# GpSimd's two-input elementwise work moved to VectorE, with new durations and priorities in the list scheduler

## The chip, the cores and the metric

The kernel runs on one core of a Trainium2 chip. A core has TensorE (matmuls, PE in the profile), VectorE (DVE), ScalarE (ACT), GpSimd (POOL) and SyncE (SP, which here issues every DMA). The metric is the time of one execution on the device in microseconds, as the median of several runs; lower is better.

## The reference

Three parts follow each other on 4 batches of 768 tokens with 8 heads of 48, which make a model width of 384. The first is an attention whose state decays by a complex number for each token and channel:

```python
mag = np.sqrt(a_re * a_re + a_im * a_im)
scale = np.minimum(mag, 0.999) / (mag + 1e-06)
for t in range(S):
    new_re = ar * S_re - ai * S_im
    new_im = ar * S_im + ai * S_re
    kv = np.einsum('bhd,bhe->bhde', k[:, :, t], v[:, :, t])
    S_re, S_im = (new_re + kv, new_im)
    y[:, :, t] = np.einsum('bhd,bhde->bhe', q[:, :, t], S_re)
```

The second mixes tokens by a product of rank 32 and applies a two-layer network of inner width 1536; the third gates by a causal convolution of 5 taps:

```python
h = xt @ U @ V
u = x + h.transpose(0, 2, 1)
x = u + np.maximum(u @ w_ch1, 0.0) @ w_ch2
gate = 1.0 / (1.0 + np.exp(-gate_pre))
out = gate * (x @ w_val) @ w_out
```

## The kernel before

**Recording and ordering.** `chunked_path` doesn't emit instructions as it is written. It records every instruction in a `Program` with its engine (V, G, A, P and S for VectorE, GpSimd, ScalarE, TensorE and SyncE), its inputs and outputs and an estimated duration. `order` then makes a list schedule: on the engine that is free first it takes the most urgent of what is ready. Urgency is the length of the remaining work, plus a number from the table `URGE` for the part of the program and the engine. `HOP` holds the estimated gaps between engines. The order of the planned starts becomes the program, and each engine runs its list strictly in that order. So the estimates cost no time themselves, but they decide who stands in front of whom. A two-input instruction `tt` of n elements a partition is planned at 142 + 2.1 n ns on GpSimd and 69 + n / 0.96 ns on VectorE.

**Attention.** A batch is taken in three units of 256 tokens (offsets 0, 256 and 512 in names such as `xa_1_256`). In each the decay is normalised (`xa`), prefix products are made by a row of `s` and `z` steps, and the two blocks of 8 tokens are then rotated: a product goes into `xc` (written `y2` in the code), two more into `z`, and a sum of both back into `z`. A later product of q and `z` goes into `xc` too (`qh`). Then come transposes (`pst`), scores (`pss`), masking (`mt`), state (`pkv`, `st`) and output (`py`).

**MoE.** Each batch has two halves of 384 tokens (names such as `xt_0_1` are batch and half). The matmuls run in a mode with truncated inputs, so every operand is split into a large and a small part by `pair`: ScalarE copies the large part, and a subtraction makes the small one. That happens to `m3u` (the input), `m3x` (the sum after the two layers), `m3g` (the gated value), three 128x384 tiles each, and to the 30 tiles of weights (`w`), after VectorE has made singles of doubles (`wt`). Between `px` (second layer) and `pv` (value product) lie VectorE's sum into `xt` and 12 steps `g` of the convolution. The `hp` tiles (hidden layer) are made by ScalarE and VectorE alone.

**Who does what.** Four constants choose an engine by batch: the rotation's product (`JE`) and the product with q (`QE`) go to GpSimd for batches 0 and 1; the subtraction of `pair` (`LE`) goes to GpSimd for batches 0 to 2; all of the weights' (`WE`) go to GpSimd. GpSimd else only writes constants at the start and one small memset a batch.

Of the kernel before, what the change touches and what calls it, by code (L numbers as in the profile page):

```python
# [100 lines left out]
class Program:  # L101
    """Records instructions, orders them for the in-order engines, then emits them."""

    # from the end of one instruction to the start of another that needs its result
# [8 lines left out]
    # what is added to the priority of the instructions of a part of the program on an engine  # L113
    URGE = {
        "a1A": 16000.0, "a1S": -10000.0, "a1V": -168000.0, "a3A": -8000.0, "a3V": -10000.0, "m0A": -2000.0,
        "m1A": -11000.0, "m1V": 283000.0, "m2A": -4000.0, "wA": -164000.0, "wG": -18000.0, "wS": -24000.0,
        "wV": -341000.0,
    }

    def hop(self, d, u):  # L120
        return self.HOP[d.eng + u.eng] if d.eng != u.eng or u.deps[d] else 0.0
# [61 lines left out]
    # TensorE runs at half of its clock after a tick in which too few columns left the array  # L183
# [14 lines left out]
    def lay(self, urgency, back=False):  # L198
        """List schedule (from the end if back): the most urgent of what is ready on the engine that is free first."""
# [6 lines left out]
        ready = [0.0] * len(ops)  # L206
# [53 lines left out]
# ---------------------------------------------------------------- the general path  # L260
def general_path(tc, q, k, v, a_re, a_im, moe_U, moe_V, w1, w2, w_val, conv_w, w_out, out):
    """Token by token, as the recurrence says; for decays and weights outside of what the chunked path may take."""
# [15 lines left out]
    with ExitStack() as ctx:  # L278
# [7 lines left out]
        with tc.tile_pool(name="ga", bufs=1) as ap, tc.tile_pool(name="gb", bufs=2) as bp:  # L286
# [10 lines left out]
            with tc.For_i(0, S, TB) as t0:  # L297
# [8 lines left out]
                # a min(|a|, .999) / (|a| + 1e-6); zero where |a|^2 overflows  # L306
# [44 lines left out]
        # weights: doubles to singles; beyond float32's range to zero and to infinity  # L351
# [121 lines left out]
# ---------------------------------------------------------------- the kernel  # L473
# [10 lines left out]
def chunked_path(ctx, tc, outer, q, k, v, a_re, a_im, moe_U, moe_V, w1, w2, w_val, conv_w, w_out, out):  # L484
    """Attention in chunks and the rest; returns 1 where the inputs allow it."""
# [36 lines left out]
    # instructions  # L522
# [56 lines left out]
    def matmul(o, lhsT, rhs, start=True, stop=True):  # L579
        n, m = rhs.free, lhsT.free  # L580
        passes = 1 if lhsT.probe.dtype == F32R else 4
        cost = 3 + (n / 2.4 if passes == 1 else max(n / 0.6, m / 0.6))
        op = g.add(
            "P", cost, lambda: nc.tensor.matmul(real(o), real(lhsT), real(rhs), start=start, stop=stop),  # L584
            views(lhsT, rhs), [o],
        )
        op.cols = passes * n * lhsT.shape[0] / 128
        return op

    def matmuls(o, parts, cost):  # L590
        """Products into disjoint columns of the array, side by side: (where in o, lhsT, rhs, start, stop)."""
# [17 lines left out]
    def dma(o, a, slow=1.0):  # L609
        """Slow: runs of less than 512 bytes."""  # L610
# [13 lines left out]
    JE, QE, LE, WE = ("GGVV", "GGVV", "GGGV", "G")  # L624
    # constants
# [28 lines left out]
    # weights  # L654
# [7 lines left out]
    def single(t, st):  # L662
        """t = float32 of the doubles in st (low word, high word), truncated to 24 bits."""
# [40 lines left out]
    def load_weights():  # L704
        """The doubles come to where their large and small parts will be."""
# [12 lines left out]
        for i, (to, key, *_) in enumerate(todo):  # L718
            x = T("p3", [128, PW], F32, "g", f"wt{i}")
            single(x, raw[i])  # L720
            to[key] = T("wts", [128, 2, PW], F32R, f"w{i}", f"w{i}")
            act(to[key][:, 0], x)
            sub(WE, to[key][:, 1], x, f32(to[key][:, 0]))

    xts, xus, yds, state, carry = {}, {}, {}, {}, {}
    # heads in pairs, each in 64 places: v, state and transposed output
# [9 lines left out]
    def attention(b, u0, R):  # L736
# [9 lines left out]
        # before the first MoE its places are free  # L746
# [4 lines left out]
        # normalisation of a  # L751
# [3 lines left out]
        for jb in range(NB):  # L755
# [4 lines left out]
            # a s, s = min(|a|, .999) / (|a| + 1e-6) = min(1, .999 r) (1 - 1e-6 r), r = 1 / |a|  # L760
# [18 lines left out]
        # prefix products inside the blocks of a row  # L779
# [12 lines left out]
        # products of rows as columns  # L792
# [14 lines left out]
        # (re, im) and (-im, re): what the parts of another factor are multiplied by  # L807
# [4 lines left out]
        # exclusive prefix over the rows; the unit starts from the phase of all before it  # L812
# [26 lines left out]
        # magnitude of the whole, and its phase as the next seed  # L839
# [30 lines left out]
        # P = prefix products; q P and -k / conj(P)  # L870
# [6 lines left out]
        for jb, (fj, fr, fi) in enumerate(fs_):  # L877
# [8 lines left out]
            mul(JE[b], y2, fj.unsqueeze(1).to_broadcast(ms), z[:, :, 1:2, :].to_broadcast(ms))  # L886
# [11 lines left out]
            mul(QE[b], qh, qk[:, 0].unsqueeze(2).to_broadcast(ms), z)  # L898
            mul("V", z, x0.unsqueeze(2).to_broadcast(ms), z)
            dma(kd[:, j0 * P2 : (j0 + RB) * P2], z.rearrange("p j c d -> p (j c d)"))  # L900
            # rows to columns
# [9 lines left out]
        # scores, state, output of each chunk  # L911
# [64 lines left out]
        # x^T U, a quarter of the columns in each group of lanes  # L976
# [19 lines left out]
    def pair(b, src, name, where=("p3", "m3")):  # L996
        t = T(where[0], [128, 2, TT], F32R, where[1], "m3" + name)
        act(t[:, 0], src)
        sub(LE[b], t[:, 1], src, f32(t[:, 0]))
        return t[:, 0], t[:, 1]  # L1000

    def moe(b):
# [106 lines left out]
    g.add("A", 1283.0, lambda: nc.scalar.preload_act_table_set(LN_EXP), [], [])  # L1109
    load_small()  # L1110
    def attend(b):
        g.kind = f"a{b}"
        t0 = 0
        for r in UNITS[b]:
# [11 lines left out]
    # the sum of all flags; anything but zero asks for the general path  # L1126
# [54 lines left out]
```

## Time and profile before

| | us |
|---|---|
| runs | 807.25, 811.2, 812.7; median 811.2 |
| span of the profiled execution | 805.2 |
| median of the runs less the span | 6.0 |
| VectorE busy | 652.5 |
| TensorE busy | 644.8 |
| ScalarE busy | 443.9 |
| GpSimd busy | 172.8 |

The time of the profiled execution itself is not listed beside the runs, so its span, with 6.0 us around it, stands for the median. An engine's busy time is the union of its instructions' spans; two instructions that follow each other on VectorE overlap by some tens of nanoseconds, so that durations add up to more than the busy time. TensorE's busy time includes stretches in which its clock was granted at less than full speed.

### The profile page before, as it was taken

Reading aid. Unit: us, or ns where it says so; the run is one execution under the profiler, and the core shown is the slowest. Engines: PE = TensorE matmul, PEld = TensorE weight load, DVE = VectorE, ACT = ScalarE, POOL = GpSimd, SP = SyncE. Lnnn points to the kernel's source line nnn. Section 1 sums busy time; section 2 is a strip of 40 time slices with the busy share of each in tenths; the row PEclk is TensorE's granted clock in tenths of the full one; section 3 lists DMA queues with packets and bytes.
Section 4 is the critical chain, followed back from the end, with each engine's and each line's share of the span. In section 5 each row is a group of like instructions: output and inputs, shape, how many; then the busy total and the mean of one; then the engine's idle time right before and its main releaser. Section 6 shows DMA issues by size and latency. Waiting matters only on the chain. (4 is left out here: it accounts for less than half of the span.)

```text
span 805.2 us, 12333 instructions
## 1 busy us (share of the span) xinstructions
PE 644.8 (80%) x4314; PEld 585.4 (73%) x4314; DVE 652.5 (81%) x1425; ACT 443.9 (55%) x1100; POOL 172.8 (21%) x139
## 2 busy tenths in 40 slices
PE   0001777858897699987998899889988999999985
PEld 0001666746787598885997799869977999799984
DVE  4989998999998988988989998999999837414361
ACT  6777875655365454575646654756466326413243
POOL 1363425225345412131003100220042003000000
PEclk9999755786999798998999999989999999999997
DMA  7687422530121324223212434131223330200000
GB/s 193 159 238 277 123 78 63 147 87 21 59 79 41 108 70 118 79 60 99 77 61 55 133 93 134 40 99 56 63 59 119 81 96 11 70 1 1 1 30 34
DMA packets 86885, 68.72 MB, mean 85 GB/s; under 512 B 52000, under 2 KB 79648, under 8 KB 86816
## 3 DMA queue, kind: packets, MB, share of 16 engines
q1 hardware_dynamic: 86816, 67.86, 29.2%
q8 instruction: 36, 0.59, 0.3%
q14 instruction: 33, 0.27, 0.1%
HBM read 48.97 MB, written 18.87 MB: 84 GB/s over the span
## 5 line engine op out<-in xcount | busy, mean ns | idle before, releaser
L584 PE MATMUL ph<-m3u,w 128*128 128x384 f32 x864 | 225.2, 363 | 14.4 <-DVE hp L551 5.2
L584 PE MATMUL px<-hp,w 128*128 128x384 f32 x864 | 201.3, 343 | 1.6 <-ACT hp L573 1.1
L584 PEld LDWEIGHTS ph<-m3u,w 128*128 128x128 f32 x864 | 160.8, 200 | 26.2 <-POOL m3u L535 8.9
L584 PEld LDWEIGHTS px<-hp,w 128*128 128x128 f32 x864 | 153.4, 189 | 3.8 <-ACT hp L573 2.0
L573 ACT ACTIVATE hp<-ph 128x384 fp32r<-128x384 f32 x96 | 46.6, 487 | 112.0 <-PE ph L584 111.6
L551 DVE SCALAR_TENSOR_TENSOR hp<-ph,hp 128x384 fp32r<-128x384 f32 x96 | 52.8, 551 | 59.6 <-ACT hp L573 59.3
L535 POOL TENSOR_TENSOR m3x<-xt,m3x 128x384 fp32r<-128x384 f32 x18 | 25.2, 1422 | 217.0 <-ACT m3x L573 211.4
L584 PE MATMUL pss<-qT,kT 96*128 96x128 f32 x384 | 61.3, 310 | 9.0 <-ACT qT L573 6.1
L535 DVE TENSOR_TENSOR s<-xa,z 128x192 f32<-128x192 f32 x168 | 63.9, 413 | 2.2 <-ACT z L573 1.4
L584 PEld LDWEIGHTS pss<-qT,kT 96*128 96x128 f32 x384 | 56.2, 219 | 12.4 <-ACT qT L573 7.3
L535 POOL TENSOR_TENSOR w<-wt,w 128x384 fp32r<-128x384 f32 x30 | 44.1, 1481 | 89.6 <-ACT w L573 89.6
L551 DVE SCALAR_TENSOR_TENSOR g<-xt,cw,g 128x384 f32<-128x384 f32 x96 | 62.2, 717 | 0.2 <-ACT g L573 0.2
L584 PE MATMUL pv<-m3x,w 128*128 128x384 f32 x216 | 50.4, 370 | 5.6 <-POOL m3x L535 3.3
L573 ACT ACTIVATE xa<-xa,cb 128x384 f32<-128x384 f32 x72 | 43.4, 610 | 15.9 <-DVE xa L551 10.3
L584 PE MATMUL po<-w,m3g 128*128 128x384 f32 x216 | 48.0, 354 | 3.7 <-POOL m3g L535 1.9
L605 PE MATMUL pst<-eye_r,xc 128*96 128x128 f32 x192 | 31.8, 298 | 19.9 <-POOL xc L535 19.2
L584 PEld LDWEIGHTS pv<-m3x,w 128*128 128x128 f32 x216 | 39.8, 204 | 8.7 <-POOL m3x L535 4.8
L605 PE MATMUL pst<-eye_r,z 128*96 128x128 f32 x192 | 31.0, 305 | 17.1 <-DVE z L535 11.9
L596 PE MATMUL py<-mt,vt 128*64 128x128 f32 x384 | 40.3, 302 | 4.1 <-DVE mt L535 3.7
L584 PEld LDWEIGHTS po<-w,m3g 128*128 128x128 f32 x216 | 37.0, 188 | 8.7 <-POOL m3g L535 3.5
L605 PEld LDWEIGHTS pst<-eye_r,xc 128*96 128x96 f32 x192 | 24.2, 138 | 23.5 <-POOL xc L535 19.3
L535 DVE TENSOR_TENSOR xa<-xa 128x384 f32<-128x384 f32 x48 | 28.4, 592 | 15.8 <-ACT xa L573 15.8
(157 smaller groups left out, 1282.3 us busy)
## 6 DMA issues: line engine op xcount, KB each, us to landing
raw<-in_moe_w_ch_dram SPq DMA_DIRECT2D x24, 384.0 KB
kd<-z SPq DMA_DIRECT2D x24, 384.0 KB
ks<-kd SPq DMA_DIRECT2D x20, 384.0 KB
ab<-in_a_re_dram SPq DMA_DIRECT2D x24, 192.0 KB
ab<-in_a_im_dram SPq DMA_DIRECT2D x24, 192.0 KB
qk<-in_k_dram SPq DMA_DIRECT2D x24, 192.0 KB
qk<-in_q_dram SPq DMA_DIRECT2D x24, 192.0 KB
vt<-in_v_dram SPq DMA_DIRECT2D x24, 192.0 KB
```

Of the source, the lines that this page charges most:

```text
L535: e, cost, lambda: engines[e].tensor_tensor(out=real(o), in0=real(a), in1=real(b), op=op), views(a, b), [o]
L551: lambda: nc.vector.scalar_tensor_tensor(out=real(o), in0=real(a), scalar=real(s), in1=real(b), op0=o0, op1=o1),
L573: return nc.scalar.activation(real(o), real(a), func, scale=real(scale), **kw)
L584: "P", cost, lambda: nc.tensor.matmul(real(o), real(lhsT), real(rhs), start=start, stop=stop),
L596: r = nc.tensor.matmul(ro[idx], real(lhsT), real(rhs), start=start, stop=stop)
L605: op = g.add("P", cost, lambda: nc.tensor.transpose(real(o), real(a), real(idn)), views(a, idn), [o])
```

## The change

The four constants are gone and `"V"` stands in the places where they chose: 108 two-input instructions (30 for `w`, 54 for `m3u`, `m3x` and `m3g` of batches 0 to 2, 24 for `xc` of batches 0 and 1) leave GpSimd's list for VectorE's. In the planner, a matmul of 384 columns is estimated at 174 ns where it was 163, the fp32 forms get 5 ns more, and a wait between two instructions of VectorE or of ScalarE that reuse a place counts 115 or 100 ns (`AGAIN`). The parts of the program are named more finely (a unit of attention, a half of the MoE, six weights), and `URGE` has 86 numbers for them where it had 13. Comments are gone. No instruction is added or removed, and no DMA.

```diff
+    AGAIN = {"V": 115.0, "A": 100.0}
     URGE = {
-        "a1A": 16000.0, "a1S": -10000.0, "a1V": -168000.0, "a3A": -8000.0, "a3V": -10000.0, "m0A": -2000.0,
...
+        "a00A": -3500.0, "a00P": 1500.0, "a00S": 6500.0, "a00V": 500.0, "a01A": -500.0, "a01P": -1000.0,
...
     def hop(self, d, u):
-        return self.HOP[d.eng + u.eng] if d.eng != u.eng or u.deps[d] else 0.0
+        return self.HOP[d.eng + u.eng] if d.eng != u.eng or u.deps[d] else self.AGAIN.get(d.eng, 0.0)
...
-        cost = 3 + (n / 2.4 if passes == 1 else max(n / 0.6, m / 0.6))
+        cost = 14 + n / 2.4 if passes == 1 else 8 + max(n / 0.6, m / 0.6)
...
-    JE, QE, LE, WE = ("GGVV", "GGVV", "GGGV", "G")
...
         for i, (to, key, *_) in enumerate(todo):
+            g.kind = f"w{i // 6}"
...
-            sub(WE, to[key][:, 1], x, f32(to[key][:, 0]))
+            sub("V", to[key][:, 1], x, f32(to[key][:, 0]))
...
-            mul(JE[b], y2, fj.unsqueeze(1).to_broadcast(ms), z[:, :, 1:2, :].to_broadcast(ms))
+            mul("V", y2, fj.unsqueeze(1).to_broadcast(ms), z[:, :, 1:2, :].to_broadcast(ms))
...
-            mul(QE[b], qh, qk[:, 0].unsqueeze(2).to_broadcast(ms), z)
+            mul("V", qh, qk[:, 0].unsqueeze(2).to_broadcast(ms), z)
...
-        sub(LE[b], t[:, 1], src, f32(t[:, 0]))
+        sub("V", t[:, 1], src, f32(t[:, 0]))
...
         for hf in range(NH):
             n = f"_{b}_{hf}"
+            g.kind = f"m{b}{hf}"
...
-        for r in UNITS[b]:
+        for i, r in enumerate(UNITS[b]):
+            g.kind = f"a{b}{i}"
```

The first place is the end of the second layer of MoE `_0_0` (batch 0, half 0). Before, GpSimd's list holds the small parts there, with a rotation's product of attention `_1_256` between them:

```order
L535 TENSOR_TENSOR m3x_0_0_2295<-xt_0_0_131,m3x_0_0_2295 128x384
L535 TENSOR_TENSOR m3x_0_0_2300<-xt_0_0_131,m3x_0_0_2300 128x384
L535 TENSOR_TENSOR m3x_0_0_2309<-xt_0_0_131,m3x_0_0_2309 128x384
L619 MEMSET xt_1_0_2351 128x3x4
L535 TENSOR_TENSOR xc_1_256_2406<-f3_1_256_2392,z_1_256_1833 128x8x96
L535 TENSOR_TENSOR m3g_0_0_2410<-g_0_0_2250,m3g_0_0_2410 128x384
L535 TENSOR_TENSOR m3g_0_0_2413<-g_0_0_2260,m3g_0_0_2413 128x384
L535 TENSOR_TENSOR m3g_0_0_2424<-g_0_0_2269,m3g_0_0_2424 128x384
```

and VectorE's list has the sum into `xt` and the convolution's steps, one behind the other:

```order
L535 TENSOR_TENSOR xt_0_0_131<-xt_0_0_131,px2_0_0_1738 128x384
L551 SCALAR_TENSOR_TENSOR g_0_0_2250<-xt_0_0_131,cw_308,g_0_0_2250 128x384
L551 SCALAR_TENSOR_TENSOR g_0_0_2260<-xt_0_0_131,cw_308,g_0_0_2260 128x384
L551 SCALAR_TENSOR_TENSOR g_0_0_2250<-xt_0_0_131,cw_308,g_0_0_2250 128x384
L551 SCALAR_TENSOR_TENSOR g_0_0_2269<-xt_0_0_131,cw_308,g_0_0_2269 128x384
L551 SCALAR_TENSOR_TENSOR g_0_0_2250<-xt_0_0_131,cw_308,g_0_0_2250 128x384
L551 SCALAR_TENSOR_TENSOR g_0_0_2260<-xt_0_0_131,cw_308,g_0_0_2260 128x384
L551 SCALAR_TENSOR_TENSOR g_0_0_2269<-xt_0_0_131,cw_308,g_0_0_2269 128x384
L551 SCALAR_TENSOR_TENSOR g_0_0_2260<-xt_0_0_131,cw_308,g_0_0_2260 128x384
L551 SCALAR_TENSOR_TENSOR g_0_0_2269<-xt_0_0_131,cw_308,g_0_0_2269 128x384
```

Now GpSimd's list holds only constants and memsets, and at the same place on VectorE the three subtractions stand among the convolution's steps:

```order
L551 TENSOR_TENSOR xt_0_0_92<-xt_0_0_92,px2_0_0_1751 128x384
L567 SCALAR_TENSOR_TENSOR g_0_0_2234<-xt_0_0_92,cw_336,g_0_0_2234 128x384
L567 SCALAR_TENSOR_TENSOR g_0_0_2238<-xt_0_0_92,cw_336,g_0_0_2238 128x384
L567 SCALAR_TENSOR_TENSOR g_0_0_2234<-xt_0_0_92,cw_336,g_0_0_2234 128x384
L567 SCALAR_TENSOR_TENSOR g_0_0_2238<-xt_0_0_92,cw_336,g_0_0_2238 128x384
L567 SCALAR_TENSOR_TENSOR g_0_0_2234<-xt_0_0_92,cw_336,g_0_0_2234 128x384
L567 SCALAR_TENSOR_TENSOR g_0_0_2238<-xt_0_0_92,cw_336,g_0_0_2238 128x384
L551 TENSOR_TENSOR m3x_0_0_2241<-xt_0_0_92,m3x_0_0_2241 128x384
L551 TENSOR_TENSOR m3x_0_0_2244<-xt_0_0_92,m3x_0_0_2244 128x384
L567 SCALAR_TENSOR_TENSOR g_0_0_2248<-xt_0_0_92,cw_336,g_0_0_2248 128x384
L567 SCALAR_TENSOR_TENSOR g_0_0_2234<-xt_0_0_92,cw_336,g_0_0_2234 128x384
L567 SCALAR_TENSOR_TENSOR g_0_0_2248<-xt_0_0_92,cw_336,g_0_0_2248 128x384
```

The first two `m3x` follow the sixth step of the convolution, the third follows the eleventh.

The second place is the rotation of attention `_1_256` on VectorE. Before, its product into `xc` was GpSimd's, and VectorE's list reads:

```order
L535 TENSOR_TENSOR t1_1_256_2426<-f3_1_256_2392,z_1_256_1833 128x192
L535 TENSOR_TENSOR xa_1_512_2046<-ab_1_512_2196,xa_1_512_2046 128x8x96
L535 TENSOR_TENSOR z_1_256_1833<-f3_1_256_2392,z_1_256_1833 128x8x48 x2
L535 TENSOR_TENSOR fb_1_256_2454<-t1_1_256_2426 128x96
L535 TENSOR_TENSOR z_1_256_1833<-z_1_256_1833,xc_1_256_2406 128x768
```

Now the products into `xc` of both blocks stand among the others:

```order
L551 TENSOR_TENSOR xc_1_256_2413<-f3_1_256_2386,z_1_256_1771 128x8x96
L551 TENSOR_TENSOR st0_132<-pkv_1_0_1_2400,st1_128 96x8x48
L551 TENSOR_TENSOR t1_1_256_2426<-f3_1_256_2386,z_1_256_1771 128x192
L567 SCALAR_TENSOR_TENSOR xa_1_512_2048<-xa_1_512_2048 128x8x48
L551 TENSOR_TENSOR z_1_256_1771<-f3_1_256_2386,z_1_256_1771 128x8x48
L551 TENSOR_TENSOR fb_1_256_2438<-t1_1_256_2426 128x96
L551 TENSOR_TENSOR z_1_256_1771<-f3_1_256_2386,z_1_256_1771 128x8x48
L551 TENSOR_TENSOR xa_1_512_2048<-ab_1_512_2227,xa_1_512_2048 128x8x96
L551 TENSOR_TENSOR xc_1_256_2459<-fb_1_256_2438,z_1_256_1771 128x8x96
L551 TENSOR_TENSOR xt_0_1_1656<-xt_0_1_1656,pu_0_1_2472 128x384
L551 TENSOR_TENSOR z_1_256_1771<-z_1_256_1771,xc_1_256_2413 128x768
```

Two products of 128x768 have moved in between (`xc` from `f3` and from `fb`), ahead of the sum that reads the first of them.

On TensorE's list the order of the stages stays: the first matmul of MoE `_0_0` stands 50.2 us of matmul work from the list's start in both kernels and the first of MoE `_3_0` 484.8 us, where work is counted as each matmul by the shortest duration of its form in the trace.

## Rows read from the trace of the kernel before

**Rows 1.** The page: busy time, share of the span and instructions of each engine.

```profile
PE 644.8 (80%) x4314; PEld 585.4 (73%) x4314; DVE 652.5 (81%) x1425; ACT 443.9 (55%) x1100; POOL 172.8 (21%) x139
```

**Rows 2.** Windows: length, then PE, PEld, DVE, ACT, POOL busy, clock, DMA share, GB/s.

```profile
0.00:190.00 190.00, 86.12 (x555) 71.23 (x555) 169.73 (x393) 128.51 (x367) 70.95 (x66) 0.81 0.51 147
190.00:690.00 500.00, 456.67 (x3187) 415.67 (x3186) 436.58 (x939) 274.42 (x643) 101.84 (x74) 0.96 0.27 77
690.00:806.00 116.00, 102.03 (x574) 98.48 (x573) 46.16 (x95) 40.98 (x92) 0.00 (x0) 0.96 0.07 22
620.00:690.00 70.00, 69.10 (x544) 64.43 (x542) 40.64 (x79) 28.08 (x57) 6.64 (x6) 1.00 0.23 64
```

**Rows 3.** GpSimd's groups by form: count, busy us, mean ns, idle before, releasers.

```profile
L535 POOL TENSOR_TENSOR m3x<-xt,m3x 128x384 fp32r<-128x384 f32 x18 | 25.2, 1422 | 217.0 <-ACT m3x L573 211.4 <-DVE g L551 5.6
```

**Rows 4.** Timeline at 274 us: start, duration, engine, instruction.

```profile
274.43 1.82 POOL L535 TENSOR_TENSOR xc<-qk,z 128x768 f32<-128x768 f32 x1 [1.24 <-DVE xc L551]
...
274.74 1.73 DVE L535 TENSOR_TENSOR z<-s,s 128x192 f32<-128x192 f32 x1
```

**Rows 5.** VectorE's groups by form, whole run.

```profile
L535 DVE TENSOR_TENSOR s<-xa,z 128x192 f32<-128x192 f32 x168 | 63.9, 413 | 2.2 <-ACT z L573 1.4
...
L551 DVE SCALAR_TENSOR_TENSOR g<-xt,cw,g 128x384 f32<-128x384 f32 x96 | 62.2, 717 | 0.2 <-ACT g L573 0.2
...
L551 DVE SCALAR_TENSOR_TENSOR hp<-ph,hp 128x384 fp32r<-128x384 f32 x96 | 52.8, 551 | 59.6 <-ACT hp L573 59.3
...
L535 DVE TENSOR_TENSOR z<-s,s 128x192 f32<-128x192 f32 x84 | 35.7, 425 | 0.6
...
L535 DVE TENSOR_TENSOR z<-xc,z 128x768 f32<-128x768 f32 x24 | 23.6, 984 | 3.6 <-POOL xc L535 3.4
...
L535 DVE TENSOR_TENSOR z<-f,z 128x384 f32<-128x384 f32 x24 | 20.3, 844 | 3.7 <-POOL xc L535 3.4
...
L535 DVE TENSOR_TENSOR m3u<-xt,m3u 128x384 fp32r<-128x384 f32 x6 | 3.3, 554 | 1.6 <-ACT m3u L573 1.6
...
L563 DVE TENSOR_SCALAR fine<-f 1x1 int32<-1x1 f32 x1 | 0.1, 142 | 7.1 <-ACT f L573 7.1
```

**Rows 6.** VectorE's groups by form, 380 to 420 us, where GpSimd is idle.

```profile
L551 DVE SCALAR_TENSOR_TENSOR hp<-ph,hp 128x384 fp32r<-128x384 f32 x12 | 6.6, 548 | 0.2 <-ACT hp L573 0.2
...
L535 DVE TENSOR_TENSOR s<-xa,z 128x192 f32<-128x192 f32 x14 | 4.5, 352 | 0.8 <-ACT z L573 0.6
...
L535 DVE TENSOR_TENSOR z<-s,s 128x192 f32<-128x192 f32 x7 | 2.5, 353 | 0.2
...
L535 DVE TENSOR_TENSOR xc<-qk,z 128x768 f32<-128x768 f32 x2 | 1.9, 958 | 0.1
...
L535 DVE TENSOR_TENSOR z<-f,z 128x384 f32<-128x384 f32 x1 | 0.5, 546 | 0.0
```

**Rows 7.** VectorE's groups by form, 740 to 790 us, after GpSimd's last instruction.

```profile
L551 DVE SCALAR_TENSOR_TENSOR g<-xt,cw,g 128x384 f32<-128x384 f32 x23 | 12.5, 612 | 0.0
```

**Rows 8.** TensorE's groups by form, whole run.

```profile
L584 PE MATMUL ph<-m3u,w 128*128 128x384 f32 x864 | 225.2, 363 | 14.4 <-DVE hp L551 5.2 <-POOL m3u L535 4.7 <-ACT m3u L573 4.0
...
L584 PE MATMUL pv<-m3x,w 128*128 128x384 f32 x216 | 50.4, 370 | 5.6 <-POOL m3x L535 3.3 <-DVE m3x L535 1.3 <-ACT ob L573 0.8
...
L584 PE MATMUL po<-w,m3g 128*128 128x384 f32 x216 | 48.0, 354 | 3.7 <-POOL m3g L535 1.9 <-ACT m3g L573 1.7
```

**Rows 9.** Timeline around the end of `px` of MoE `_0_0`.

```profile
242.25 6.43 DVE L551 SCALAR_TENSOR_TENSOR g<-xt,cw,g 128x384 f32<-128x384 f32 x12
...
245.43 6.61 POOL L535 TENSOR_TENSOR m3x<-xt,m3x 128x384 fp32r<-128x384 f32 x3 [6.30 <-ACT m3x L573]
...
249.59 2.29 PE L584 MATMUL pv<-m3x,w 128*128 128x384 f32 x6 [3.31 <-POOL m3x L535]
```

**Rows 10.** The chain that ended last, near 715 us: start, us, what.

```profile
713.50 0.52 PE px L584 x3
```

**Rows 11.** Timeline at 185 us: the first layer of MoE `_0_0` begins.

```profile
185.68 4.53 PE L584 MATMUL ph<-m3u,w 128*128 128x384 f32 x13 [1.24 <-POOL m3u L535]
```

More of the change, by code (lines that the diff above doesn't have):

```diff
@@ L111 @@
     }
+    AGAIN = {"V": 115.0, "A": 100.0}
     URGE = {
-        "a1A": 16000.0, "a1S": -10000.0, "a1V": -168000.0, "a3A": -8000.0, "a3V": -10000.0, "m0A": -2000.0,
-        "m1A": -11000.0, "m1V": 283000.0, "m2A": -4000.0, "wA": -164000.0, "wG": -18000.0, "wS": -24000.0,
-        "wV": -341000.0,
[16 rows of a table added]
     }
     def hop(self, d, u):
-        return self.HOP[d.eng + u.eng] if d.eng != u.eng or u.deps[d] else 0.0
+        return self.HOP[d.eng + u.eng] if d.eng != u.eng or u.deps[d] else self.AGAIN.get(d.eng, 0.0)
     def __init__(self, nc):
@@ L1109, in chunked_path @@
     g.add("A", 1283.0, lambda: nc.scalar.preload_act_table_set(LN_EXP), [], [])
+    g.kind = "s"
     load_small()
     def attend(b):
-        g.kind = f"a{b}"
         t0 = 0
-        for r in UNITS[b]:
+        for i, r in enumerate(UNITS[b]):
+            g.kind = f"a{b}{i}"
             attention(b, t0, r)
```

15 rows, old and new, of the table URGE are left out of this document.

## The prediction

> **What bounds the kernel now.** I read the page's shares first, then windows by stage, then the groups of GpSimd and VectorE, then the timeline where both work. By the page no engine is full: VectorE 81%, TensorE 80%, GpSimd 21% [rows 1]. By stages it looks different [rows 2]. Up to 190 us (weights and the first attention) VectorE is busy for 169.7 of 190 us and TensorE for 86.1: VectorE sets the end of this stage. From 690 us (the MoE of batch 3) TensorE is busy for 102.0 of 116 us, and VectorE for 46.2: TensorE sets it. In the middle, 500 us long, TensorE has 456.7 and VectorE 436.6; there they take turns, and only its last 70 us are plainly TensorE's (69.1 of 70). The middle is where an idle TensorE can be won back: it has 43.3 us without a matmul, and a granted clock of 0.96.
>
> The second thing to see is that VectorE's own durations are not constant. At 274.43 us GpSimd begins a product of 1.82 us; a VectorE sum `z<-s,s` that begins 0.3 us later lasts 1.73 us and ends with it, within a quarter of a microsecond [rows 4]. In a stretch without work on GpSimd that same form takes 353 ns [rows 6]. Over the whole run forms with two SBUF inputs are longer than in quiet stretches: `s` 413 against 352 ns, `z<-s,s` 425 against 353, `z<-f,z` 844 against 546 [rows 5, 6], `g` 717 against 612 [rows 5, 7]. `hp`, which reads one input from PSUM, keeps its 551 against 548 [rows 5, 6]. So a GpSimd instruction often holds up one VectorE instruction until it ends, where both read two tensors in SBUF.
>
> The Trainium skill says the same of the cause (SBUF — State Buffer, Who interferes with whom): a VectorE instruction with two SBUF inputs and a GpSimd instruction that reads SBUF contend for one shared port, and whichever comes second is blocked wholly. By that rule, the trace agrees, 1.73 us for the blocked sum.
>
> **The change, part by part.**
>
> *What VectorE gains back.* Four forms alone: `s` 168 x (413 - 352) = 10.2 us, `g` 96 x (717 - 612) = 10.1, `z<-s,s` 84 x (425 - 353) = 6.0, `z<-f,z` 24 x (844 - 546) = 7.2, in sum 33.6 [rows 5 to 7]. The same subtraction over all 57 forms (1425 instructions, from `s` to `fine` [rows 5]), each against the median of its instructions that no GpSimd arithmetic overlaps, gives 79 us: 27 in instructions that start before 190 us, 53 in the middle, nothing after. That is 0.73 us for each of GpSimd's 108 two-input instructions.
>
> *What VectorE gets.* 84 subtractions of 128x384 at 554 ns (the six that VectorE did already [rows 5]) are 46.5 us; 24 products of 128x768 at 958 ns [rows 6] are 23.0. Neighbours overlap: all durations add up to 739 us where VectorE was busy for 652.5 [rows 1], which is 0.06 us for each of 1425. So 69.5 - 108 x 0.06 = 63.0 us of new busy time. Net: 63 - 79 = -16 us; VectorE's work becomes smaller though it takes over GpSimd's.
>
> *First stage.* Ahead of the first `xt` sum of MoE `_0_0`, VectorE's new list holds 46 more instructions, 29.0 us by their durations, 26 after overlap; 27 come back. Its waits for GpSimd's products ahead of `z`, 3.4 and 3.4 us [rows 5], vanish as waits, since the products are its own now. The weight loads are issued in another order and the V tables first; VectorE has other work meanwhile, and I cost that at nothing (without this cover it is the few DMA issues that move ahead, some 2 us). In sum -6 or so; I take -5.
>
> *Middle.* 63 - 26 = 37 us come, 53 go: -16 on VectorE in 500 us. It shows only where VectorE is the later one; the bounds are 0 and all 16. TensorE has 43.3 us without a matmul and is otherwise busy, so I take two thirds, -11.
>
> *Boundaries of the MoE.* 18 groups of three subtractions (`m3u`, `m3x`, `m3g`, two halves, three batches) stand between ScalarE's large part and TensorE. In MoE `_0_0` the three took GpSimd 6.61 us beside the twelve `g`, and TensorE waited 3.31 us for the second of them [rows 9]. In the new order two stand behind the sixth `g` and one behind the eleventh: 13 instructions of some 0.53 us (6.43 us for twelve [rows 9]) and the third is done 7 us after the first `g` begins, where it was 9.8 (245.43 + 6.61 - 242.25). By the means [rows 3, 5] a group lasts 3 x 0.55 = 1.7 us in place of 3 x 1.42 = 4.3 (`m3x`'s mean). Fully exposed that were 18 x 2.6 = 47 us; TensorE's waits that name GpSimd come to 4.7 + 3.3 + 1.9 = 9.9 us [rows 8], the other bound is 0, where each subtraction waits behind VectorE's instruction in progress as long as it gains. I take -7, near the waits.
>
> *Planner.* The old table planned a matmul of 384 columns at 163 ns; the chain shows three in 0.52 us, 173 each [rows 10], the new estimate. VectorE's plan held no blocking at all, so 79 us of its time fell outside the plan, and what stood next in its list need not have been what TensorE missed most. What a plan that fits better is worth the profile of before doesn't show; bounds are +15 (an order fitted to the plan and not to the chip) and -15 (about a third of the 43.3 us [rows 2]). I take -3.
>
> *Last stage.* Batch 3's subtractions were VectorE's already and TensorE sets the pace: 0. The lists of TensorE differ there only in how `pv` and `po` of one half stand among the other's matmuls.
>
> Sum: -5 - 11 - 7 - 3 = -26 us. The span of 805.2 stands for the median of 811.2, with 6.0 around it; so **785 us**.
>
> **The rivals.**
>
> *More: the idle time in the middle is halved* (chance 0.18). If all of VectorE's 16 us show, the waits of 9.9 us go, the first stage gives 6 and the plan and the clock (0.96 over 500 us [rows 2]) another 14, that is -46: 765. For it: where TensorE idles in the middle, VectorE is mostly busy. Against: both were near full, and only one order can suit both.
>
> *Hidden* (0.12). TensorE holds the middle and VectorE's relief turns into idle time. For it: the last 70 us of the middle [rows 2]. Against: 43.3 us without a matmul. Between -10 and 0: 801 to 811, about 808.
>
> *Slower, by the queue on VectorE* (0.05). GpSimd could start a subtraction as soon as ScalarE's part was there; on VectorE it stands at a planned place behind the convolution or a unit of attention. Place: the same 18 groups. Price: if each comes as much as 2.8 us later (five `g` of 0.54 us in front, as before the third `m3x`), 18 x 2.8 = 50 us, 811 - 26 + 50 = 835. It decides from 26 / 18 = 1.4 us a group. Against: in the place that I followed the third came earlier.
>
> *Slower, because VectorE is full* (0.05). If its long instructions had another cause than GpSimd, nothing comes back and 63 us come on top. VectorE is idle for 20 us in the first stage and 63 in the middle [rows 2], of which 29 lie in the last 70 us; with some 28 of the 63 us taken up there, 35 remain: 846. It decides where less than about half of the 79 us comes back. Against: `hp` does not lengthen.
>
> The Trainium skill has a rule that leans this way (Perfetto Trace Analysis, Optimizing Scalar/DVE Operations): where VectorE is saturated, moving work to other engines, even to GpSimd, may make sense; it adds that between these two it might not help, because of the port. Taken alone, the first half speaks for the old split.
>
> That the change does not do what it says is excluded: the new list has the 108 on VectorE and only memsets and constants on GpSimd.
>
> **How the numbers follow.** Forecast 785 (0.60, by itself 773 to 797), more 765 (0.18), hidden 808 (0.12), the two slower ones 0.05 each. A change of 1% (8 us) is about what a measurement of this kernel can tell. Faster by over 1%: 0.60 + 0.18 + a third of the hidden case, 0.82. Within 1%: the rest of it and the edge of the slower ones, 0.09. Slower: 0.09. The range leaves out about 0.07 below, and above it the slower cases and a little of the hidden one: 765 to 806.
>
> **What would show it.** VectorE's busy time falls to some 636 us with 108 more instructions; `s`, `g` and `z` come to 352, 612 and 350 to 546 ns everywhere. The first layer of MoE `_0_0` begins at about 181 us, where it was 185.7 [rows 11]. TensorE's idle time in the middle falls below 30 us, and the stage from 190 to 690 us shrinks to about 480. The last stage stays at 116. I am wrong if VectorE's durations stay long without GpSimd, if new waits of TensorE for `m3u`, `m3x` or `m3g` on VectorE pass 25 us, or if the middle keeps its length with VectorE idler.

## The result and the profile after

The changed kernel takes 775.11 us (median of 4 runs, 772.76 to 778.13) where the kernel before took 809.23 beside it (4 runs): ratio 0.9572, 95% interval 0.9533 to 0.9611. Its profiled execution took 775.49 us with a span of 773.7, so that 1.8 us lie around the span.

Page of after, first part, for [rows 1]:

```profile
PE 627.6 (81%) x4314; PEld 578.4 (75%) x4314; DVE 626.0 (81%) x1533; ACT 442.7 (57%) x1100; POOL 2.7 (0%) x31
```

VectorE executes 108 more instructions and is busy for 26.5 us less; GpSimd falls from 172.8 to 2.7 us. TensorE is busy for 17.2 us less with the same 4314 matmuls.

Windows of after, for [rows 2], same columns:

```profile
0.00:190.00 190.00, 82.92 (x556) 69.89 (x557) 166.73 (x442) 131.93 (x374) 2.33 (x28) 0.82 0.51 147
190.00:690.00 500.00, 473.07 (x3364) 438.20 (x3363) 425.42 (x1027) 280.45 (x662) 0.32 (x3) 0.98 0.28 79
```

Between 190 and 690 us TensorE has 26.9 us without a matmul, where it had 43.3, and fits 177 matmuls more into the same 500 us.

VectorE's groups of after by form, whole run, for [rows 5]:

```profile
L551 DVE TENSOR_TENSOR s<-xa,z 128x192 f32<-128x192 f32 x168 | 54.8, 355 | 4.3 <-ACT z L589 3.9
L567 DVE SCALAR_TENSOR_TENSOR g<-xt,cw,g 128x384 f32<-128x384 f32 x96 | 53.1, 617 | 0.2 <-ACT g L589 0.2
L567 DVE SCALAR_TENSOR_TENSOR hp<-ph,hp 128x384 fp32r<-128x384 f32 x96 | 53.0, 554 | 59.1 <-ACT hp L589 58.5
...
L551 DVE TENSOR_TENSOR z<-s,s 128x192 f32<-128x192 f32 x84 | 29.9, 355 | 0.3
...
L551 DVE TENSOR_TENSOR z<-f,z 128x384 f32<-128x384 f32 x24 | 13.3, 553 | 0.0
```

Every form has in the whole run, to about 1%, the duration that it had before in stretches without GpSimd [rows 6, 7]; `hp` stays where it was.

TensorE's groups of after by form, for [rows 8]:

```profile
L600 PE MATMUL ph<-m3u,w 128*128 128x384 f32 x864 | 215.0, 355 | 8.5 <-ACT m3u L589 3.9 <-DVE hp L567 3.0 <-DVE m3u L551 1.3
...
L600 PE MATMUL pv<-m3x,w 128*128 128x384 f32 x216 | 53.0, 372 | 6.4 <-DVE m3x L551 3.6 <-ACT m3x L589 2.0 <-ACT ob L589 0.8
L600 PE MATMUL po<-w,m3g 128*128 128x384 f32 x216 | 51.1, 355 | 0.0
```

The waits for a small part came to 9.9 us on GpSimd; on VectorE they are 1.3 + 3.6 + 0. Of the 3.6 us, 1.4 belong to batch 3, whose small parts were VectorE's already and cost 1.3 us then [rows 8]; for batches 0 to 2 it is 9.9 us before and 3.5 after.

**Where the time went.** I cut the spans where TensorE has done the same work in both kernels, to a few matmuls, and to whole microseconds: up to the first layer of MoE `_0_0`; from there to that of `_1_0`; to that of `_3_0`; to the end. Windows of before:

```profile
0.00:181.00 181.00, 79.47 (x537) 65.89 (x537) 160.76 (x377) 125.22 (x358) 63.90 (x61) 0.82 0.53 152
181.00:374.00 193.00, 166.46 (x1080) 148.80 (x1080) 177.20 (x381) 104.64 (x255) 63.47 (x41) 0.90 0.26 74
374.00:695.00 321.00, 300.61 (x2153) 274.71 (x2153) 271.33 (x586) 176.78 (x409) 45.42 (x38) 0.98 0.27 78
695.00:805.00 110.00, 98.29 (x545) 95.98 (x545) 43.17 (x84) 37.27 (x81) 0.00 (x0) 0.96 0.05 18
```

and of after:

```profile
0.00:185.00 185.00, 77.92 (x538) 65.04 (x539) 161.73 (x427) 128.63 (x367) 2.33 (x28) 0.83 0.53 151
185.00:350.00 165.00, 152.10 (x1081) 139.41 (x1082) 157.48 (x396) 102.60 (x248) 0.11 (x1) 0.98 0.30 85
350.00:664.00 314.00, 299.97 (x2155) 278.23 (x2155) 264.11 (x630) 174.92 (x408) 0.22 (x2) 0.97 0.29 81
664.00:774.00 110.00, 97.58 (x544) 95.71 (x542) 42.63 (x83) 36.56 (x80) 0.00 (x0) 0.95 0.04 14
```

The first stretch became 4 us longer, the second 28 shorter, the third 7 shorter; the last kept its length. The 28 have two halves: TensorE is idle for 12.9 us instead of 26.5, and busy for 152.1 instead of 166.5 with the same matmuls, at a granted clock of 0.98 instead of 0.90.

### The profile page after: what moved, and what is told of

Its sections match the earlier page's. It is cut to its first block, busy times and chain, and to the rows that moved or that the text cites. A ratio compares the mean times of both kernels' runs of the same rounds, so it can differ in the third digit from the quotient of the medians.

```text
span 773.7 us, 12227 instructions
## 1 busy us (share of the span) xinstructions
PE 627.6 (81%) x4314; PEld 578.4 (75%) x4314; DVE 626.0 (81%) x1533; ACT 442.7 (57%) x1100; POOL 2.7 (0%) x31
## 4 chain that ended last, share of the span: by engine, by line
PE 48%; DVE 25%; DMA 13%; ACT 7%; issue 3%; SPq 2%; ACTq 0%; DVEq 0%
PE ph L600 14%; PE px L600 12%; DMA ab<-in_a_im_dram 5%; PE pv L600 5%; DVE xc L551 4%; PE py L612 4%; DVE z L551 4%; PE pss L600 3%; PE po L600 3%; PE pkv L612 3%; DVE g L567 3%; DVE s L551 3%; DVE xa L551 2%; DMA raw<-in_moe_w_ch_dram 2%; SPq L631 2%
## 5 line engine op out<-in xcount | busy, mean ns | idle before, releaser
L600 PE MATMUL ph<-m3u,w 128*128 128x384 f32 x864 | 215.0, 355 | 8.5 <-ACT m3u L589 3.9
L600 PE MATMUL px<-hp,w 128*128 128x384 f32 x864 | 206.2, 344 | 0.2 <-ACT hp L589 0.2
L600 PE MATMUL pss<-qT,kT 96*128 96x128 f32 x384 | 59.0, 301 | 5.2 <-ACT qT L589 5.2
L551 DVE TENSOR_TENSOR s<-xa,z 128x192 f32<-128x192 f32 x168 | 54.8, 355 | 4.3 <-ACT z L589 3.9
L600 PE MATMUL pv<-m3x,w 128*128 128x384 f32 x216 | 53.0, 372 | 6.4 <-DVE m3x L551 3.6
L567 DVE SCALAR_TENSOR_TENSOR g<-xt,cw,g 128x384 f32<-128x384 f32 x96 | 53.1, 617 | 0.2 <-ACT g L589 0.2
L600 PE MATMUL po<-w,m3g 128*128 128x384 f32 x216 | 51.1, 355 | 0.0
L621 PE MATMUL pst<-eye_r,xc 128*96 128x128 f32 x192 | 31.8, 293 | 19.9 <-DVE xc L551 17.2
L621 PE MATMUL psT<-eye_r,qd 128*96 128x128 f32 x24 | 5.3, 305 | 45.8 <-ACT qd L589 43.0
L612 PEld LDWEIGHTS pkv<-vt,ks 128*96 128x96 f32 x320 | 34.5, 188 | 5.4 <-issue 3.8
L589 ACT ACTIVATE xa<-ab 128x768 f32<-128x768 f32 x24 | 20.2, 842 | 31.3 <-DMA ab<-in_a_im_dram 21.9
```

Of the source, the lines that this page charges most:

```text
L551: e, cost, lambda: engines[e].tensor_tensor(out=real(o), in0=real(a), in1=real(b), op=op), views(a, b), [o]
L567: lambda: nc.vector.scalar_tensor_tensor(out=real(o), in0=real(a), scalar=real(s), in1=real(b), op0=o0, op1=o1),
L589: return nc.scalar.activation(real(o), real(a), func, scale=real(scale), **kw)
L612: r = nc.tensor.matmul(ro[idx], real(lhsT), real(rhs), start=start, stop=stop)
L621: op = g.add("P", cost, lambda: nc.tensor.transpose(real(o), real(a), real(idn)), views(a, idn), [o])
```

## The experiments

Theory A (the prediction's): GpSimd's two-input instructions held up VectorE's, and without them VectorE's time comes back, whatever the plan. B: the new plan makes the gain. C: the small parts come later because of VectorE's queue, and something else makes up for it. D: the small parts reach TensorE sooner because VectorE needs 0.55 us for one. Ratios are to the kernel before, run beside each on the same chip; "lengthening" is the sum over VectorE's instructions of their duration less the median of those of the same form that no GpSimd arithmetic overlaps, 79 us before and 0 after.

**e1_old_order_on_dve.** The kernel before with its own plan; only the engine that executes the 108 is another, each at the place where its planned start put it.

```diff
-            e, cost, lambda: engines[e].tensor_tensor(out=real(o), in0=real(a), in1=real(b), op=op), views(a, b), [o]
+            e, cost, lambda: nc.vector.tensor_tensor(out=real(o), in0=real(a), in1=real(b), op=op), views(a, b), [o]
```

> The kernel before with its plan and the lists of TensorE, ScalarE and SyncE untouched; the 108 two-input instructions that were GpSimd's stand at the same places of the program but are VectorE's. If the blocking by GpSimd is what was lost (theory A), VectorE's forms come to their quiet durations (s 352, g 612 ns), its busy time falls by 10 to 25 us, and the time comes to 785 to 797 although nothing was planned for it. If the new plan is what gained (rival B), the time stays at 805 to 815. If VectorE's queue is a loss that the plan has to hide (rival C), it is above 820.

Measured: 776.91 us, ratio 0.9598 [0.9542, 0.9655], lengthening 0, VectorE busy for 630.9 us. Windows, cut as above:

```profile
0.00:172.00 172.00, 75.87 (x537) 63.22 (x537) 155.35 (x408) 125.01 (x358) 2.34 (x28) 0.92 0.56 160
172.00:354.00 182.00, 164.06 (x1080) 148.50 (x1080) 166.27 (x423) 105.61 (x256) 0.11 (x1) 0.90 0.27 78
354.00:670.00 316.00, 299.88 (x2154) 275.28 (x2155) 266.47 (x623) 177.12 (x410) 0.22 (x2) 0.98 0.28 80
```

The move alone gives the whole gain within the intervals, and 8 us more than A expected at best; B falls as its cause. The way there is another: the first stretch gets 9 us shorter and not 4 longer, the second 11 and not 28, and the clock of the second stays at 0.90.

**e2_new_order_on_gpsimd.** The changed kernel's plan, with the 108 executed by GpSimd at the places that the plan gave them on VectorE.

```diff
-        cost = 142 + 2.1 * n if e == "G" else 69 + n / 0.96
+        cost = 69 + n / 0.96
-            e, cost, lambda: engines[e].tensor_tensor(out=real(o), in0=real(a), in1=real(b), op=op), views(a, b), [o]
+            "V", cost, lambda: engines[e].tensor_tensor(out=real(o), in0=real(a), in1=real(b), op=op), views(a, b), [o]
...
-            sub("V", to[key][:, 1], x, f32(to[key][:, 0]))
+            sub("G", to[key][:, 1], x, f32(to[key][:, 0]))
...
-        sub("V", t[:, 1], src, f32(t[:, 0]))
+        sub("GGGV"[b], t[:, 1], src, f32(t[:, 0]))
```

> The changed kernel with its plan and the lists of TensorE, ScalarE and SyncE untouched; the same 108 instructions go back to GpSimd at their places. Theory A: VectorE's two-input forms lengthen by some 60 to 80 us in all, TensorE waits for m3u, m3x and m3g on GpSimd, and the time comes to 800 to 825. Rival B: it stays at 773 to 785, since the order is the new one. Rival C: it is at or under 775, since VectorE has 63 us less to do.

Measured: 810.43 us, ratio 1.0023 [0.9986, 1.006], lengthening 71 us. The new order without the move is worth nothing; the move on it is worth 1.0023 - 0.9572 = 0.045, on the old order 0.040.

**e3_move_replanned.** The kernel before with `"V"` in the four constants, planned anew with the old durations and priorities.

```diff
-    JE, QE, LE, WE = ("GGVV", "GGVV", "GGGV", "G")
+    JE, QE, LE, WE = ("VVVV", "VVVV", "VVVV", "V")
```

> The kernel before with its four constants set to VectorE, planned again with the old durations and old priorities. Theory A: 780 to 797, most of the gain. Rival B: 803 to 815.

Measured: 836.90 us, ratio 1.0336 [1.0298, 1.0374], with lengthening 0; neither A nor B had expected a loss of this size. It shows most in the stretch from MoE `_0_0` to `_0_1`:

```profile
175.00:303.00 128.00, 106.96 (x617) 96.50 (x617) 121.86 (x315) 72.49 (x176) 0.11 (x1) 0.76 0.25 74
```

It was 90 us long before and 73 after. VectorE, busy for 121.9 of the 128 us, is given work of attention in front of MoE `_0_1`: 318.8 us of its durations start ahead of that first layer, in the changed kernel 281.6. TensorE has work of other parts in the stretch too, 617 matmuls where before has 447, so that not all of its length is lost. Over equal work the loss is spread: from `_0_0` to `_1_0` it takes 216 us (193 before, 182 in e1), from there to `_3_0` 334 us (321 and 316). The same move that gains 4% on the old order loses 3% when the planner may react to it with this table.

**e4_plan_only.** The changed kernel's durations and priorities with the four constants of before, planned anew.

```diff
-            sub("V", to[key][:, 1], x, f32(to[key][:, 0]))
+            sub("G", to[key][:, 1], x, f32(to[key][:, 0]))
...
-            mul("V", y2, fj.unsqueeze(1).to_broadcast(ms), z[:, :, 1:2, :].to_broadcast(ms))
+            mul("GGVV"[b], y2, fj.unsqueeze(1).to_broadcast(ms), z[:, :, 1:2, :].to_broadcast(ms))
...
-        sub("V", t[:, 1], src, f32(t[:, 0]))
+        sub("GGGV"[b], t[:, 1], src, f32(t[:, 0]))
```

> The changed kernel with the four constants as before (GpSimd keeps its 108 instructions), planned with the new durations and new priorities. Theory A: 795 to 815, little gain, since the blocking stays. Rival B: 775 to 787.

Measured: 842.83 us, ratio 1.0436 [1.0398, 1.0474], lengthening 71 us. B as a gain of the plan by itself falls once more. A's range is missed as well: with the same lengthening the time is 32 us above e2, so that the rest of the loss is this plan's.

**e5_gpsimd_repeats_subs.** The changed kernel with its lists; behind each of 84 subtractions (those of `w` and of batches 0 to 2) GpSimd repeats it on the last 32 lanes, and nothing reads the result. So the blocking is put back, and little else of the old split.

```diff
+    def sub2(o, a, b):
+        def fn():
+            cut = lambda x: real(x[96:].rearrange("p (x y) -> p x y", y=64))
+            r = nc.vector.tensor_tensor(out=real(o), in0=real(a), in1=real(b), op=ALU.subtract)
+            nc.gpsimd.tensor_tensor(out=real(spare), in0=cut(a), in1=cut(b), op=ALU.subtract)
+            return r
```

> The changed kernel with the same lists on TensorE, VectorE, ScalarE and SyncE; behind 84 of the moved subtractions (30 of the weights, 54 of the MoE) GpSimd does the same subtraction once more on the last 32 lanes, and nothing reads the result. So the work and its way stay, and GpSimd's reads come back. Theory A, blocking: VectorE's forms with two SBUF inputs lengthen by 40 to 65 us in all and the time comes to 793 to 812. Rival D, the shorter way of the subtractions is the gain: 773 to 781.

Measured: 816.08 us, ratio 1.0128 [1.0092, 1.0164]; VectorE's durations add up to 776.8 us where after has 734.0, and the lengthening is 49 us. Its groups by form, and GpSimd's largest:

```profile
L576 DVE SCALAR_TENSOR_TENSOR g<-xt,cw,g 128x384 f32<-128x384 f32 x96 | 60.7, 691 | 0.2 <-ACT g L598 0.2
L551 DVE TENSOR_TENSOR s<-xa,z 128x192 f32<-128x192 f32 x168 | 58.3, 374 | 0.4
```

```profile
L558 POOL TENSOR_TENSOR st<-wt,w 32x384 f32<-32x384 f32 x30 | 81.4, 2713 | 150.5 <-ACT w L598 122.9 <-DVE xa L576 18.6 <-DVE wt L576 4.5
```

Work whose result nobody uses takes all of the gain back, with `g` and `s` long again: A. The time is somewhat above A's upper end. A rival is that the repeats, which last 2.7 us in the mean for `w`, hold their inputs' places for so long. The waits in the trace that name a repeat are small: VectorE's for the places of `wt`, 4.5 us in all, and none of TensorE's.

**e6_gpsimd_copies.** As e5, but GpSimd copies one of the two inputs.

```diff
-            nc.gpsimd.tensor_tensor(out=real(spare), in0=cut(a), in1=cut(b), op=ALU.subtract)
+            nc.gpsimd.tensor_copy(real(spare), cut(a))
```

> As the run before, but GpSimd copies the one input instead of subtracting two. If any read of SBUF by GpSimd holds VectorE up, VectorE's forms lengthen in proportion to the copies' durations, and the time lies between 775 and that of the run before. If only GpSimd's two-input instructions hold it up, VectorE's durations stay at their quiet values and the time at 773 to 781.

Measured: 783.08 us, ratio 0.9714 [0.9686, 0.9741]; VectorE's durations add up to 739.5 us, 5.5 above after. VectorE's `g` and GpSimd's largest group by form:

```profile
L576 DVE SCALAR_TENSOR_TENSOR g<-xt,cw,g 128x384 f32<-128x384 f32 x96 | 54.5, 624 | 0.2 <-ACT g L598 0.2
```

```profile
L558 POOL COPY st<-wt 32x384 f32<-32x384 f32 x30 | 48.3, 1609 | 173.7 <-DVE wt L576 141.9 <-DVE cx L551 24.3 <-DVE s L551 3.5
```

The sum of durations understates the lengthening: after's own 734.0 us are 5.2 above e1's, with the same instructions and no GpSimd arithmetic in either. As defined above it is 12 us, where e5 has 49, and the time lies between after and e5, as it should if any read of SBUF by GpSimd holds VectorE up. The other theory, that only two inputs do, wanted quiet durations and at most 781 us. Timeline of e6:

```profile
354.77 0.51 POOL L558 COPY st<-xt 32x384 f32<-32x384 f32 x1 [0.80 <-DVE xt L551]
354.83 0.85 DVE L557 TENSOR_TENSOR m3u<-xt,m3u 128x384 fp32r<-128x384 f32 x1
...
356.15 0.55 DVE L557 TENSOR_TENSOR m3u<-xt,m3u 128x384 fp32r<-128x384 f32 x1
```

The `m3u` beside the copy lasts 0.30 us longer than the next one. Beside 38 of the 84 copies a VectorE instruction is over 0.2 us longer than its form's median in after, by 0.34 us at most; beside the repeats of e5 it is 74 of 84, and 0.83 us at most. The loss of time falls alike, to a quarter (0.0142 against 0.0556). What makes a copy cheaper isn't its number of inputs alone: the shortest copy takes 0.51 us and the shortest repeat 0.99, and a copy begins without ScalarE's large part, so at another moment. No run changes one of the three alone.

**e7_old_order_subs_on_dve and e8_old_order_rest_on_dve.** The two halves of e1, each on the lists of before: e7 moves the 54 subtractions of the MoE, e8 the 30 of the weights and the 24 products. In e7 (in e8 the same for the other three lines):

```diff
+    def tt_v(e, o, a, b, op):
+        n = o.free
+        cost = 142 + 2.1 * n if e == "G" else 69 + n / 0.96
+        return g.add(
+            e, cost, lambda: nc.vector.tensor_tensor(out=real(o), in0=real(a), in1=real(b), op=op), views(a, b), [o]
+        )
...
-        sub(LE[b], t[:, 1], src, f32(t[:, 0]))
+        tt_v(LE[b], t[:, 1], src, f32(t[:, 0]), ALU.subtract)
```

> The kernel before with its lists untouched, but only the 54 subtractions of the MoE (m3u, m3x, m3g of batches 0 to 2) are executed by VectorE. Theory A: VectorE gets 27 us and some 39 come back; with the boundaries the time comes to 786 to 798, about half of the gain of moving all. Rival D: nearly all of it, 776 to 784.

> The kernel before with its lists untouched, but only the other 54 instructions (30 of the weights, 24 products of the rotation) are executed by VectorE. Theory A: VectorE gets 36 us and some 40 come back, mostly before 300 us; 788 to 800. Rival D: 803 to 813.

Measured: e7 789.69 us, ratio 0.9787 [0.9761, 0.9814], lengthening 45 us; e8 792.39 us, ratio 0.9821 [0.9794, 0.9847], lengthening 34 us. The gains add up: 0.0213 + 0.0179 = 0.0392, e1 had 0.0402; 45 + 34 = 79 us, all of the lengthening of before. VectorE's forms of e7:

```profile
L558 DVE SCALAR_TENSOR_TENSOR g<-xt,cw,g 128x384 f32<-128x384 f32 x96 | 53.1, 611 | 0.2 <-ACT g L580 0.2
L535 DVE TENSOR_TENSOR z<-f,z 128x384 f32<-128x384 f32 x24 | 22.5, 939 | 3.7 <-POOL xc L535 3.4
```

and of e8:

```profile
L558 DVE SCALAR_TENSOR_TENSOR g<-xt,cw,g 128x384 f32<-128x384 f32 x96 | 62.2, 718 | 0.2 <-ACT g L580 0.2
L535 DVE TENSOR_TENSOR z<-f,z 128x384 f32<-128x384 f32 x24 | 13.2, 551 | 0.2
```

Each form is long beside just that GpSimd work which stands beside it in the lists: `g` beside `m3x`, `z` beside the products into `xc`. D, which expected nearly all of the gain from the MoE's 54 and none from the other 54, can't be the whole cause, since the others give nearly as much. What it can be worth is a small part: for batches 0 to 2 TensorE's waits for a small part are 9.9 us before and 5.1 in e1, a fall of 5 us where e1 gains 31.

**e9_no_again, e10_old_matmul_estimates, e11_no_priorities, e12_move_no_priorities.** What the table and the durations are worth. Each is planned anew: e9 without `AGAIN`, e10 with the old estimates of a matmul, e11 with an empty `URGE`; e12 is e3 with an empty `URGE`. Theory N: a table of priorities fits one set of durations only.

```diff
-    AGAIN = {"V": 115.0, "A": 100.0}
+    AGAIN = {}
```

```diff
-        cost = 14 + n / 2.4 if passes == 1 else 8 + max(n / 0.6, m / 0.6)
+        cost = 3 + (n / 2.4 if passes == 1 else max(n / 0.6, m / 0.6))
```

```diff
-    URGE = {
...
-    }
+    URGE = {}
```

> The changed kernel, planned without the 100 and 115 ns for two instructions of one engine that reuse a place (the table of priorities kept); VectorE's list has 283.2 us of work ahead of MoE _0_1's first layer where the changed kernel's has 276.6. Theory N (the table of priorities belongs to one set of durations, and each other set gives a plan that is worse by an amount that has little to do with the size of the estimate changed): 10 to 60 us above the changed kernel, so 785 to 835, with the loss visible as a later start of some MoE half, and VectorE's durations unchanged (s 355, g 617 ns). Rival (the estimates matter by themselves and little): within 5 us of the changed kernel, 770 to 780.

> The changed kernel, planned with the old estimates of a matmul (163 ns for 384 columns where it has 174), table of priorities kept; VectorE's list has 268.5 us of work ahead of MoE _0_1's first layer, less than the changed kernel's 276.6. Theory N: 10 to 60 us above the changed kernel, 785 to 835. Rival (the 11 ns a matmul matter little by themselves): 770 to 780.

> The changed kernel, planned with an empty table of priorities, durations as changed: urgency is then the remaining work alone. It gives the level from which the 86 numbers start. VectorE's list has 296.4 us of work ahead of MoE _0_1's first layer (changed kernel 276.6, the kernel before's unfitted replan 317.0). Theory N: an empty table does no worse than a table fitted to other durations, 800 to 835, so a gain of 25 us or more belongs to the fitted table alone. Rival (the table is worth little): 775 to 785.

> The kernel before with the 108 instructions on VectorE in the plan too (old estimates, no 100 and 115 ns), as in the 836.9 us run, but with an empty table of priorities. The new estimates with an empty table gave 784.9. Theory N (the 836.9 came from the 13 priorities, fitted to a plan with GpSimd, and not from the old estimates): 780 to 800, with the first layer of MoE _0_1 begun before 280 us where it was 303. Rival (the old estimates make a bad plan by themselves): 820 to 840.

| | us | ratio | first layer of MoE `_0_1` at |
|---|---|---|---|
| after | 775.11 | 0.9572 [0.9533, 0.9611] | 257.8 |
| e9, without `AGAIN` | 790.08 | 0.9793 [0.975, 0.9836] | 262.5 |
| e10, old matmul estimates | 787.87 | 0.9757 [0.97, 0.9814] | 251.2 |
| e11, empty table | 784.87 | 0.974 [0.968, 0.98] | 272.4 |
| e12, empty table, old durations | 800.11 | 0.9873 [0.981, 0.9936] | 280.8 |
| e3, old table, old durations | 836.90 | 1.0336 [1.0298, 1.0374] | 303.1 |

In all of them the lengthening is 0, so that the differences are of the order alone. The fitted table is worth 1.7% over none (e11), and with one estimate changed by 11 ns, or one term left out, it is no better than none (e9, e10): N holds there, near the lower end of what it expected. The later start that it wanted to see is there in e9; e10 begins `_0_1` earlier than after and only `_1_0` later (354.4 against 349.7). e11 fell at the upper end of the rival's range and not in N's: an empty table is a better start than N had it. e12 came out at N's upper edge, far from the rival's 820. The old table with the move is worse than none by 4.6% (e12 against e3), and the old durations cost 1.3% with no table in either (e12 against e11).

## Why the prediction was right, point by point

The forecast was 785 us, -26 from its base; 775.1 was measured, -34 from 809.2. The direction and the mechanism held; several of its sizes did not.

**The blocking: right in kind and in size.** The prediction put 79 us of VectorE's time down to GpSimd and expected durations of 739 + 69.5 - 79 = 729.5 us in sum; e1, which changes nothing else, has 728.8. Busy it is for 630.9 us there, where 652.5 - 16 = 636 was forecast, and for 626.0 after. That it is GpSimd's work beside VectorE's, and not another effect of the move, is shown by e5.

**The first stage: right for the move, wrong for the kernel.** -5 was forecast; with the old order it is -8.7 (first layer of MoE `_0_0` at 172.5 us), and in the changed kernel +3.6 (184.8). The prediction also misread its reference: it took 185.7 us, the start of a later batch of 13 matmuls [rows 11]; the first `ph` of before stands at 181.2. VectorE's busy time up to there came out about as worked out from the lists, 161.7 against 160.8 us. The step that failed is that 6.8 us of waits for GpSimd's products would vanish and nothing follow: VectorE idles for 23.3 us there, where it did for 20.2 (16.6 in e1). VectorE's waits in after, up to 185 us (waiting for what: us in total, times, longest):

```profile
DVE xa L551 <- ACT xa L589: 5.7, 5, 2.5
DVE vt L579 <- DMA vs<-in_moe_V_dram: 4.9, 2, 4.4
DVE s L551 <- ACT z L589: 3.9, 1, 3.9
DVE st L551 <- PE pkv L612: 2.7, 1, 2.7
```

and the same view of before:

```profile
DVE xa L535 <- ACT xa L573: 9.4, 2, 6.4
DVE z L535 <- POOL xc L535: 6.8, 4, 1.7
DVE vt L563 <- DMA vs<-in_moe_V_dram: 1.0, 2, 0.6
```

The products' 6.8 us are gone, but the V tables, whose earlier place I costed at nothing (2 us without cover), are now waited for 4.9 us where it was 1.0, and two more waits of 3.9 and 2.7 us for ScalarE and TensorE are new: the plan's, since in e1 none of the three passes 0.2 us.

**The middle: undersized.** From the first layer of MoE `_0_0` to that of `_3_0` it was 514.2 us (181.2 to 695.4) and is 478.9: -35, where the middle, the boundaries and the planner had -11 - 7 - 3 = -21. With the old order it is -17 against -11 - 7 = -18, which is right. By the spans of the profiled executions the terms of the move were thus well sized here; by the medians the whole move is worth -31 us (808.4 to 776.9), where its terms had -5 - 11 - 7 = -23, and by the profiled spans -27, since that execution of e1 (780.0 us) is one of its slower ones. The plan's term was not well sized: in the middle it is another -18, in the first stage +12, at the end +1.5. In sum that is -5 by the three spans and -2 by the medians (776.9 to 775.1, intervals overlapping), so that -3 was right by luck: a loss that was not seen cancels a gain that was not seen. Most of the -18 lies in the second stretch, where TensorE's busy time falls from 164.1 (e1) to 152.1 us at a clock of 0.98 instead of 0.90. No step of the forecast had a term for the clock; its rival of 765 us named it. Its two levels are 1.2 and 2.4 GHz, so that 0.90 and 0.98 are means of a stretch; what raised it no run here takes apart, since every plan that changed it changed the gaps between matmuls too (26.5 us without a matmul in before, 12.9 in after). Fewer gaps did not raise it in e1, which has 17.9 us of them and stays at 0.90. Part of it can be chance, since one kernel's clock differs from run to run: e1 was granted 0.923 to 0.956 over the span in its four runs, and after, with 0.935, has less than e1's profiled run with 0.947.

**The boundaries: the waits fell by about -7.** In MoE `_0_0` the place came out as worked out from the lists. Timeline of after, start and duration:

```profile
232.05 3.26 DVE L567 SCALAR_TENSOR_TENSOR g<-xt,cw,g 128x384 f32<-128x384 f32 x6
...
235.22 1.02 DVE L551 TENSOR_TENSOR m3x<-xt,m3x 128x384 fp32r<-128x384 f32 x2
...
235.83 4.01 PE L600 MATMUL pv<-m3x,w 128*128 128x384 f32 x14 [2.20 <-DVE m3x L551]
236.16 2.73 DVE L567 SCALAR_TENSOR_TENSOR g<-xt,cw,g 128x384 f32<-128x384 f32 x5
...
238.81 0.55 DVE L551 TENSOR_TENSOR m3x<-xt,m3x 128x384 fp32r<-128x384 f32 x1
```

The third small part is done 7.3 us after the first `g` begins (7 forecast, 9.8 before [rows 9]). TensorE still waits here, 2.20 us for the first two, which stand behind six `g`. Over batches 0 to 2 the waits for small parts fell from 9.9 to 3.5 us (5.1 in e1), so by 6.4 where -7 was forecast. The waits for ScalarE's large parts stayed, 5.7 us before and 5.9 after.

**The base.** With 1.8 us around the span, as in the other profiled runs, the profiled execution of before took some 807.0 us and not 811.2; from there the same sum gives 781. That is 4 of the 10 us by which the forecast was too high.

**The last stage** stayed: 110 us in both windows.

**The rivals.** "Hidden" fell: TensorE's idle time in the middle went from 43.3 to 26.9 us. The queue on VectorE (835) fell: the waits that it would cause are 4.9 us in all. "VectorE is full" (846) fell with the durations: all of the 79 us came back. That the planner could turn the move into a loss was the planner's bound of +15; e3 shows that a plan not fitted to the move costs 60 us against e1.

## What to carry to other kernels

Before work is given to GpSimd "because it is idle", compare the durations of VectorE's two-input instructions beside GpSimd's work and in a quiet stretch: here 108 GpSimd instructions cost VectorE 79 us, more than the 63 us that it needs to do them itself. Separate an edit from its plan by executing it at unchanged places of the list first (e1): the same move was worth -4% there, +3% with a table fitted to something else and -1% with none. A fitted table of priorities is part of one set of estimates, and is fitted again, or emptied, when any of them changes.

## What the runs showed of the hardware that was not expected

**GpSimd waits far longer than VectorE does.** Timeline of e5 with two repeats of the subtraction, and VectorE beside them:

```profile
71.50 22.11 POOL L558 TENSOR_TENSOR st<-wt,w 32x384 f32<-32x384 f32 x2 [7.62 <-ACT w L598]
...
79.26 0.54 DVE L551 TENSOR_TENSOR xc<-xc 128x384 f32<-128x384 f32 x1
...
80.47 0.55 DVE L551 TENSOR_TENSOR xc<-xc 128x384 f32<-128x384 f32 x1
```

For 22 us GpSimd got through two instructions, 7.8 and 14.2 us long, while VectorE's, one behind the other, kept their 0.54 us. The shortest repeat takes 0.99 us, and the longest delay of a VectorE instruction in this run is 0.83 us. I read it so that who has the reads keeps them as long as its next instruction is there in time, and that VectorE is held up only where GpSimd gets in; no run tests that by itself.

**A copy on GpSimd holds VectorE up too, for less.** The Trainium skill (SBUF — State Buffer, Who interferes with whom) says that a VectorE instruction with two SBUF inputs contends with any GpSimd instruction that reads SBUF, and that the loser is blocked wholly. The traces agree with both kinds: the lengthening is 49 us for 84 subtractions (e5), 0.58 us each, and 12 us for 84 copies (e6), 0.14 us each. But a GpSimd instruction beside VectorE's isn't always paid for by VectorE. Timeline of e6:

```profile
63.37 5.32 POOL L558 COPY st<-wt 32x384 f32<-32x384 f32 x1 [3.00 <-DVE wt L576]
...
63.70 0.34 DVE L551 TENSOR_TENSOR s<-xa,z 128x192 f32<-128x192 f32 x1
63.97 0.94 DVE L551 TENSOR_TENSOR xc<-f,z 128x768 f32<-128x768 f32 x1
64.84 0.34 DVE L551 TENSOR_TENSOR t<-f,z 128x192 f32<-128x192 f32 x1
```

This copy lasts 5.32 us, and none of these three is longer than alone. Whether a one-input copy on 128 lanes would cost VectorE as little was not tried.
